# Two moves between VectorE and GpSimd in the second half of a fused attention and two-FFN kernel

## The chip, the cores and the metric

The kernel runs on one core of one Trainium2 chip. The metric is device time in microseconds (us). Four engines matter here: TensorE (PE in the profile's rows) multiplies into PSUM, its weight loads stand as PEld; ScalarE (ACT), VectorE (DVE) and GpSimd (POOL) work on tiles of 128 partitions; SyncE (SP) issues the transfers.

## The reference

`attn(q, k, v)` normalises q and k over 6016 tokens, makes a 256 x 256 softmax over channels and applies it to v. Two feed-forward layers follow, each 256 to 2048 to 256 for 6016 tokens:

```python
h = x @ w_in;  g = h * np.cos(h);                    x = g @ w_out    # first layer
h = x @ w_in;  g = h * (1.0 / (1.0 + np.exp(-h)));   x = g @ w_out    # second layer (SiLU)
```

## The kernel before

The program has three parts. The first (to about 70 us) makes the softmax and folds it into the first layer's w_in. The second (to about 600 us) runs the first layer over 12 blocks of tokens, 4 of 512 and 8 of 496, with 8 pairs of hidden chunks each: 96 units. The third (from about 602 us to the end) is the second layer, and all of the change lies there. Instructions are issued to each engine in the order in which the code is written, and an engine runs its own in that order. A wait is a semaphore set by another engine.

In the third part a 2 x 2 block product is made with seven products instead of eight, P1 to P7, in both directions. Each matmul operand is a pair of tiles, `hi` (rounded to fp32r) and `lo` (the rest), and each product takes three matmuls (hi hi, lo hi, hi lo). For a unit (block b, pair m) the seven products of w_in with x give, after sums in PSUM, four quadrants of h. SiLU of these is the left part of a tile `t` with 8 planes of 128 x c, where c is half a block: 256 for the first four blocks and 248 for the others. From planes 0 to 3 VectorE forms the four others: two by one instruction (line 422, `forms_first`), plane 6 (line 427, called **T3** in this text) and plane 7 (line 428, **T4**, which needs T3). Planes 1 to 7 are then split into `hi` by ScalarE (line 433) and `lo` by VectorE (line 436), each in two instructions: the raw planes 1 to 3 (128 x 3c, 744 columns at c = 248) and the formed planes 4 to 7 (128 x 4c, 992 columns). Then the seven products with w_out add up in two PSUM tiles of the block over its 8 units: the first tile holds P1, P6, P7, P4, the second P5, P3, P2.

The loop runs over slots j (lines 646 to 721), one per unit. In slot j TensorE does P4 and P5 of unit j-1, P1 and P7 of unit j, four w_out products of unit j-3, P3 of j-1, P2 and P6 of j, and the last three w_out products of j-3: 14 products, 42 matmuls. VectorE adds two seeds (lines 660, 661, from PSUM into `t`) for unit j-1, makes `lo` raw and `lo` formed of unit j-2, and then forms_first, T3 and T4 of unit j-1. ScalarE copies P1 and a seed (669, 670), takes the first SiLU (693, needs line 661), makes `hi` formed of unit j-2 (433), two more SiLUs (703, 704), a seed (706), and `hi` raw of unit j-1 (433). P3 adds into the PSUM tile that line 661 reads, so TensorE waits there for VectorE.

When the eighth unit of a block is added up (every 8 slots, here called the boundary), `emit_out` takes the sums: ScalarE copies the first PSUM tile to `q` (line 519), VectorE copies the second (lines 522, 523), and GpSimd makes seven additions within `q` (line 526) and SyncE stores the two halves (lines 530, 534). The additions stand in four steps, one after each of the next slots' T4. GpSimd has no other work in the third part. The last block takes its sums on VectorE.

Of the kernel before, what the change touches and what calls it, by code (L numbers as in the profile page):

```python
# [15 lines left out]
ALU = mybir.AluOpType  # L16
# [47 lines left out]
def attention_then_two_ffns(ctx: ExitStack, tc: tile.TileContext, qk, vT, tau, w_in1, w_out1, w_in2, w_out2, outT):  # L64
# [6 lines left out]
    nc = tc.nc  # L71
# [175 lines left out]
    for g, n in enumerate(GROUPS):  # L247
        c0 = sum(GROUPS[:g])
        t = ep.tile([P, GMAX, 2, C], F32, tag="qk", name=f"qk{g}", bufs=8)
# [47 lines left out]
    for a in range(CH):  # L297
        nc.vector.scalar_tensor_tensor(
            out=E[:, a], in0=S[:, a, :C], scalar=rk[:, a : a + 1], in1=rq, op0=ALU.mult, op1=ALU.mult
# [80 lines left out]
    def emit_first(u, hp):  # L380
        b, m = u
        n = BLOCKS[b][1]
        t = flat(sc.tile([P, NS, HB], F32, tag="t", name=f"t1_{b}_{m}"))
        k = t.bitcast(I32)[:, :, :n]
        nc.scalar.activation(k, hp[:, :, :n], AF.Copy, scale=1.0 / TWO_PI, bias=0.25)  # L385
        nc.vector.scalar_tensor_tensor(  # L386
            out=t[:, :, :n], in0=k, scalar=-TWO_PI, in1=hp[:, :, :n], op0=ALU.mult, op1=ALU.add
        )
        return t
# [34 lines left out]
        )  # L424

    def forms_second(t, c, eng):
        eng.tensor_tensor(out=t[:, 6, :c], in0=t[:, 1, :c], in1=t[:, 5, :c], op=ALU.subtract)  # L427
        eng.tensor_tensor(out=t[:, 7, :c], in0=t[:, 3, :c], in1=t[:, 6, :c], op=ALU.subtract)

    RAW, FORMED = slice(0, 3), slice(3, NU)  # L430
# [4 lines left out]
    def part_lo(t, hi, lo, sl, c):  # L435
        nc.vector.tensor_tensor(  # L436
            out=lo[:, sl, :c], in0=t[:, 1:][:, sl, :c], in1=hi[:, sl, :c].bitcast(F32), op=ALU.subtract
        )
# [26 lines left out]
    def load_x2(b):  # L465
        c = BLOCKS[b][1] // 2
        xparts[2, b] = [xp.tile([P, NU, HB], F32R, tag=f"x{s}", name=f"x2{s}{b}") for s in ("hi", "lo")]
        for t, d in zip(xparts[2, b], xs.pop(b)):
            nc.sync.dma_start(out=t[:, :, :c].bitcast(F32), in_=d)


    def product(out, name, w, x, start, first=True, stop=True):

        ka, kb = PRODUCTS[name]
        for i, (p, r) in enumerate(PASSES):
            nc.tensor.matmul(  # L476
                out,
                w[:, p, ka - 1],
                x[r][:, kb - 1, : out.shape[-1]],
                start=(start and i == 0),  # L480
                stop=(stop and i == 2),
                skip_group_check=True,
            )
# [18 lines left out]
    def emit_out(b):  # L502

        t0, n = BLOCKS[b]
        c = n // 2
        o = state[2, b]
        last = b == NB - 1
        q = qp.tile([P, NU, HB], F32, tag="q", name=f"q{b}", bufs=1)
        p1, p6, p7, p4, p5, p3, p2 = [q[:, i, :c] for i in range(NU)]
        to = outT.rearrange("(a p) (n) -> p a n", p=P)[:, :, t0 : t0 + n].rearrange("p a (j c) -> p a j c", j=2)  # L510
        if last:

            s1, s6, s7, s4, s5, s3, s2 = [o[t][:, k, j, :c] for t, k, j in BANKS.values()]
            eng = nc.vector
            nc.scalar.activation(p1, s1, AF.Copy)
        else:
            s6, s7, s4, s5, s3, s2 = p6, p7, p4, p5, p3, p2
            eng = nc.gpsimd
            nc.scalar.activation(  # L519
                q[:, :4, :c].rearrange("p (k j) c -> p k j c", k=2), o[0][:, :, :, :c], AF.Copy  # L520
            )
            nc.vector.tensor_copy(q[:, 4:6, :c], o[1][:, 0, :, :c])
            nc.vector.tensor_copy(p2, o[1][:, 1, 0, :c])

        def add(out, x, y):
            eng.tensor_tensor(out=out, in0=x, in1=y, op=ALU.add)  # L526

        def first():
            add(p7, p7, s5)
            nc.sync.dma_start(out=to[:, 0], in_=q[:, 2:4, :c])  # L530

        def second():
            add(p2, p1, s2)
            (nc.scalar if last else nc.sync).dma_start(out=to[:, 1], in_=q[:, 5:7, :c])

        return [
            lambda: (add(p6, p1, s6), add(p7, p6, s7)),
            lambda: (add(p4, p7, s4), first()),
            lambda: (add(p6, p6, s5), add(p3, p6, s3)),
            second,  # L540
        ]


# [15 lines left out]
    def fetch(key, to):  # L559
        name, m = key  # L560
        w2[name][m] = to
        nc.sync.dma_start(out=to.bitcast(F32), in_=later.pop(key))
# [3 lines left out]
    def fetch_third():  # L566
        key = third.pop(0)
        fetch(key, as_forms(wp.tile(QUAD, F32R, tag="quad", name=f"{key[0]}_{key[1]}", bufs=8)))
# [7 lines left out]
    for i, u in enumerate(units):  # L576
# [13 lines left out]
        t = emit_first(u, hp)  # L590
# [54 lines left out]
    adds = []  # L645
    for j in range(len(units) + LAG2):
        u, p, o = [units[j - d] if 0 <= j - d < len(units) else None for d in (0, 1, LAG2)]
        if u is not None and u[1] == 2 and u[0] < NB - 1:
            load_x2(u[0] + 1)

        if p is not None:
            k = (j - 1) % 2
            c = BLOCKS[p[0]][1] // 2
            w, x = w2["wi2"][p[1]], xparts[2, p[0]]
            y, z = ys[k][:, :c], zs[k][:, :c]
            p7, u2 = seeds[j - 1]
            t = F[j - 1] = sc.tile([P, NS, HB], F32, tag="t", name=f"t2_{j - 1}")
            product(z, "P4", w, x, start=False)
            product(y, "P5", w, x, start=False)
            nc.vector.tensor_tensor(out=t[:, 1, :c], in0=z, in1=u2, op=ALU.add)  # L660
            nc.vector.tensor_tensor(out=t[:, 0, :c], in0=y, in1=p7, op=ALU.add)  # L661
        if u is not None:
            k2 = j % 2
            c2 = BLOCKS[u[0]][1] // 2
            w_, x_ = w2["wi2"][u[1]], xparts[2, u[0]]
            seeds[j] = [sp.tile([P, HB], F32, tag=s, name=f"{s}_{j}")[:, :c2] for s in ("p7", "u2")]
            product(xx[k2][:, :c2], "P1", w_, x_, start=True)
            product(zs[k2][:, :c2], "P7", w_, x_, start=False)
            nc.scalar.activation(ys[k2][:, :c2], xx[k2][:, :c2], AF.Copy)
            nc.scalar.activation(seeds[j][0], zs[k2][:, :c2], AF.Copy)  # L670
        if j - 2 in hl:
            t_, hi_, lo_, c_ = hl[j - 2]
            part_lo(t_, hi_, lo_, RAW, c_)
        if left:
            v = units[left[0]]
            emit_o1(v, parts.pop(left.pop(0)))
            if v[1] % 2 == 1:
                fetch_third()
            if v[1] == NPAIR - 1:
                steps += emit_x2(v[0])  # L680
        elif steps:
            for _ in range(min(3, len(steps))):
                steps.pop(0)()
            if not steps:
                y_room.close()
                late = ctx.enter_context(tc.tile_pool(name="late", bufs=1))
                for key in FOURTH:
                    fetch(key, late.tile([P, 2, NU, P], F32R, name=f"{key[0]}_{key[1]}"))
        names = list(BANKS)
        if o is not None:  # L690
            emit_o2(o, hl[j - LAG2][1:3], names[:4])
        if p is not None:
            nc.scalar.activation(t[:, 0:2, :c], t[:, 0:2, :c], AF.Silu)  # L693
        if j - 2 in hl:
            part_hi(t_, hi_, FORMED, c_)
            part_lo(t_, hi_, lo_, FORMED, c_)
        if p is not None:
            product(y, "P3", w, x, start=False)
        if u is not None:
            product(xx[k2][:, :c2], "P2", w_, x_, start=False)  # L700
            product(ys[k2][:, :c2], "P6", w_, x_, start=False)
        if p is not None:
            nc.scalar.activation(t[:, 3, :c], xx[k][:, :c], AF.Silu)
            nc.scalar.activation(t[:, 2, :c], y, AF.Silu)
        if u is not None:
            nc.scalar.activation(seeds[j][1], ys[k2][:, :c2], AF.Copy)
        if o is not None:
            emit_o2(o, hl.pop(j - LAG2)[1:3], names[4:])
            if o[1] == NPAIR - 1:
                adds += emit_out(o[0])  # L710
                if o[0] == NB - 1:
                    for step in adds:
                        step()
        if p is not None:
            hi, lo = [sc.tile([P, NU, HB], F32R, tag=s, name=f"{s}2_{j - 1}") for s in ("hi", "lo")]
            hl[j - 1] = (t, hi, lo, c)
            part_hi(t, hi, RAW, c)
            forms_first(t, c)
            forms_second(t, c, nc.vector)
            if adds:  # L720
                adds.pop(0)()


# [25 lines left out]
```

## Time and profile before

| | us |
|---|---|
| median of 3 runs (1133.59 to 1137.45) | 1134.57 |
| the profiled execution | 1134.77 |
| its span, first to last instruction | 1133.0 |
| TensorE busy in the span | 1081.4 (95%) |
| VectorE busy | 939.9 (83%) |
| ScalarE busy | 756.2 (67%) |
| GpSimd busy | 327.6 (29%) |

The span and the time of the same execution differ by 1.77 us. Matmuls are pipelined, so a row of one overlaps the next, and the busy time of TensorE is not its work at peak. A timeline row gives the start, the duration, engine, line, operation, output and inputs, and in brackets how long the engine had stood idle before it and what ended that. The duration of one instruction is longer than the distance to the next when the two don't depend on each other; distances are taken from starts.

### The profile page before, as it was taken

Reading aid. Unit: us, or ns where it says so; the run is one execution under the profiler, and the core shown is the slowest. Engines: PE = TensorE matmul, PEld = TensorE weight load, DVE = VectorE, ACT = ScalarE, POOL = GpSimd, SP = SyncE. Lnnn points to the kernel's source line nnn. Section 1 sums busy time; section 2 is a strip of 40 time slices with the busy share of each in tenths; the row PEclk is TensorE's granted clock in tenths of the full one; section 3 lists DMA queues with packets and bytes.
Section 4 is the critical chain, followed back from the end, with each engine's and each line's share of the span. In section 5 each row is a group of like instructions: output and inputs, shape, how many; then the busy total and the mean of one; then the engine's idle time right before and its main releaser. Section 6 shows DMA issues by size and latency. Waiting matters only on the chain.

```text
span 1133.0 us, 17045 instructions
## 1 busy us (share of the span) xinstructions
PE 1081.4 (95%) x6590; PEld 961.7 (85%) x6590; DVE 939.9 (83%) x1195; ACT 756.2 (67%) x1182; POOL 327.6 (29%) x282
## 2 busy tenths in 40 slices
PE   8888999999999999999998999999999999999997
PEld 7756788888888888888887999889989999899897
DVE  6899897887897888877675888888888888888887
ACT  6555666666666666665665777677677677778675
POOL 2268554564463564501000020220220220220220
PEclk9999999999999999999999999999999999999999
DMA  9712222324315324301275521022022022022000
GB/s 359 281 50 81 75 84 70 116 69 167 135 37 183 110 74 155 123 32 50 65 274 209 196 82 67 20 82 64 20 82 64 19 82 64 19 82 64 19 19 19
DMA packets 56528, 109.49 MB, mean 97 GB/s; under 512 B 2816, under 2 KB 37632, under 8 KB 56448
## 3 DMA queue, kind: packets, MB, share of 16 engines
q1 hardware_dynamic: 56176, 108.15, 28.1%
q8 instruction: 52, 0.85, 0.3%
q10 hardware_dynamic: 272, 0.25, 0.1%
q14 instruction: 28, 0.23, 0.1%
HBM read 68.75 MB, written 39.65 MB: 96 GB/s over the span
## 4 chain that ended last, share of the span: by engine, by line
PE 76%; DVE 15%; issue 4%; ACT 3%; DMA 1%; SPq 0%; DVEq 0%; ACTq 0%
PE o L412 21%; PE h L373 21%; PE o L476 15%; PE xz L476 9%; PE ys L476 8%; DVE t L422 2%; DVE acc L267 2%; DVE t L427 2%; ACT hi L433 2%; PE pw L334 1%; DVE t L661 1%; DVE lo L402 1%; ACT t L693 1%; DVE t L386 1%; DVE t L394 1%
## 5 line engine op out<-in xcount | busy, mean ns | idle before, releaser
L436 DVE TENSOR_TENSOR lo<-t,hi 128x744 fp32r<-128x744 f32 (+1 forms) x192 | 213.4, 1112 | 67.0 <-ACT hi L433 67.0
L476 PE MATMUL o<-hi,wo 128*128 128x248 f32 (+1 forms) x1344 | 246.1, 281 | 0.0
L526 POOL TENSOR_TENSOR q<-q 128x248 f32<-128x248 f32 (+1 forms) x77 | 76.3, 1001 | 498.7 <-ACT q L519 495.3
L476 PEld LDWEIGHTS o<-hi,wo 128*128 128x128 f32 x1344 | 207.8, 192 | 0.0
L373 PE MATMUL h<-xhi,wa 128*128 128x496 f32 (+1 forms) x768 | 206.1, 390 | 1.6 <-DVE wa L342 1.6
L412 PE MATMUL o<-hi,wo 128*128 128x496 f32 (+1 forms) x768 | 206.7, 391 | 0.0
L476 PE MATMUL o<-lo,wo 128*128 128x248 f32 (+1 forms) x672 | 189.2, 281 | 1.4 <-DVE lo L436 1.3
L433 ACT ACTIVATE hi<-t 128x744 fp32r<-128x744 f32 (+1 forms) x192 | 178.9, 932 | 13.5 <-PE o L476 11.0
L386 DVE SCALAR_TENSOR_TENSOR t<-t,h 128x992 f32<-128x992 int32 (+1 forms) x96 | 114.9, 1197 | 82.2 <-ACT t L385 81.8
L385 ACT ACTIVATE t<-h 128x992 int32<-128x992 f32 (+1 forms) x96 | 96.8, 1008 | 128.3 <-PE h L373 124.3
L373 PEld LDWEIGHTS h<-xhi,wa 128*128 128x128 f32 x768 | 144.0, 188 | 33.4 <-ACT wa L340 2.4
L412 PEld LDWEIGHTS o<-hi,wo 128*128 128x128 f32 x768 | 144.8, 189 | 30.8
L393 ACT ACTIVATE t<-t,half_pi 128x992 f32<-128x992 f32 (+1 forms) x96 | 109.1, 1136 | 66.4 <-DVE t L386 66.4
L476 PE MATMUL ys<-x2hi,wi 128*128 128x248 f32 (+1 forms) x576 | 122.5, 294 | 28.4 <-DVE t L661 25.9
L476 PE MATMUL xz<-x2hi,wi 128*128 128x248 f32 (+1 forms) x768 | 148.7, 281 | 0.0
L402 DVE TENSOR_TENSOR lo<-t,hi 128x992 fp32r<-128x992 f32 (+1 forms) x96 | 133.8, 1394 | 1.2 <-ACT hi L401 1.2
L476 PEld LDWEIGHTS o<-lo,wo 128*128 128x128 f32 x672 | 128.8, 192 | 1.9 <-DVE lo L436 1.9
L412 PE MATMUL o<-lo,wo 128*128 128x496 f32 (+1 forms) x384 | 119.5, 393 | 6.2 <-DVE lo L402 6.2
L394 DVE TENSOR_TENSOR t<-h,t 128x992 f32<-128x992 f32 (+1 forms) x96 | 115.1, 1199 | 6.9 <-ACT t L393 1.2
L476 PEld LDWEIGHTS ys<-x2hi,wi 128*128 128x128 f32 x576 | 88.8, 192 | 35.9 <-DVE t L661 29.7
L476 PEld LDWEIGHTS xz<-x2hi,wi 128*128 128x128 f32 x768 | 119.2, 192 | 0.1
L373 PE MATMUL h<-xlo,wa 128*128 128x496 f32 (+1 forms) x384 | 118.3, 389 | 0.0
(111 smaller groups left out, 1685.6 us busy)
## 6 DMA issues: line engine op xcount, KB each, us to landing
qk<-qk_dram SPq DMA_DIRECT2D x22, 512.0 KB, 7.7
raw_wo<-w_out_dram SPq DMA_DIRECT2D x16, 512.0 KB, 5.0
xshi<-yhi SPq DMA_DIRECT2D x8, 868.0 KB, 6.4
xslo<-ylo SPq DMA_DIRECT2D x8, 868.0 KB, 6.9
x2hi<-xshi SPq DMA_DIRECT2D x8, 868.0 KB, 5.2
x2lo<-xslo SPq DMA_DIRECT2D x8, 868.0 KB, 7.2
wo_dram<-stage_wo SPq DMA_DIRECT2D x7, 896.0 KB, 4.7
wo<-wo_dram SPq DMA_DIRECT2D x7, 896.0 KB, 7.5
```

The source lines that it names most:

```text
L267: nc.vector.tensor_tensor(out=acc[:, :n], in0=acc[:, :n], in1=sq[:, :n], op=ALU.add)
L373: nc.tensor.matmul(hp[:, s, :n], lhsT, rhs, start=(i == 0), stop=(i == len(todo) - 1))
L385: nc.scalar.activation(k, hp[:, :, :n], AF.Copy, scale=1.0 / TWO_PI, bias=0.25)
L386: nc.vector.scalar_tensor_tensor(out=t[:, :, :n], in0=k, scalar=-TWO_PI, in1=hp[:, :, :n], op0=ALU.mult, op1=ALU.add)
L393: nc.scalar.activation(t[:, :, :n], t[:, :, :n], AF.Sin, bias=half_pi)
L394: nc.vector.tensor_tensor(out=t[:, :, :n], in0=hp[:, :, :n], in1=t[:, :, :n], op=ALU.mult)
L402: nc.vector.tensor_tensor(out=lo[:, :, :n], in0=t[:, :, :n], in1=hi[:, :, :n].bitcast(F32), op=ALU.subtract)
L412: nc.tensor.matmul(o[:, e, :n], wo1_at(i, f)[:, e * P : (e + 1) * P], parts[k][:, s, :n], start=(f == 0 and (i, k) == PASSES[0]), stop=(f ...
L433: nc.scalar.activation(hi[:, sl, :c], t[:, 1:][:, sl, :c], AF.Copy)
L436: nc.vector.tensor_tensor(out=lo[:, sl, :c], in0=t[:, 1:][:, sl, :c], in1=hi[:, sl, :c].bitcast(F32), op=ALU.subtract)
L476: nc.tensor.matmul(out, w[:, p, ka - 1], x[r][:, kb - 1, : out.shape[-1]], start=(start and i == 0), stop=(stop and i == 2), skip_group_ch ...
L526: eng.tensor_tensor(out=out, in0=x, in1=y, op=ALU.add)
```

## The change

T4 goes from VectorE to GpSimd in all 96 slots of the third part (T3 stays on VectorE; the other use of `forms_second`, in `emit_x2` on the first layer's output, keeps both on VectorE). The seven additions of a block's sums go from GpSimd to VectorE. The two copies of the second PSUM tile leave the boundary slot: `emit_out` now returns six steps, the copies first, and the loop runs one step per slot right after lines 658 and 659 (660 and 661 before).

```diff
     def forms_second(t, c, eng):
-        eng.tensor_tensor(out=t[:, 6, :c], in0=t[:, 1, :c], in1=t[:, 5, :c], op=ALU.subtract)
+        nc.vector.tensor_tensor(out=t[:, 6, :c], in0=t[:, 1, :c], in1=t[:, 5, :c], op=ALU.subtract)
         eng.tensor_tensor(out=t[:, 7, :c], in0=t[:, 3, :c], in1=t[:, 6, :c], op=ALU.subtract)
...
-            nc.vector.tensor_copy(q[:, 4:6, :c], o[1][:, 0, :, :c])
-            nc.vector.tensor_copy(p2, o[1][:, 1, 0, :c])
+
+        def second_tile():
+            if not last:
+                nc.vector.tensor_copy(q[:, 4:6, :c], o[1][:, 0, :, :c])
+                nc.vector.tensor_copy(p2, o[1][:, 1, 0, :c])
 
         def add(out, x, y):
-            eng.tensor_tensor(out=out, in0=x, in1=y, op=ALU.add)
...
+            nc.vector.tensor_tensor(out=out, in0=x, in1=y, op=ALU.add)
+
+        def store(e, sl, eng=nc.sync):
+            eng.dma_start(out=to[:, e], in_=q[:, sl, :c])
 
         return [
+            second_tile,
             lambda: (add(p6, p1, s6), add(p7, p6, s7)),
-            lambda: (add(p4, p7, s4), first()),
+            lambda: add(p4, p7, s4),
+            lambda: (add(p7, p7, s5), store(0, slice(2, 4))),
             lambda: (add(p6, p6, s5), add(p3, p6, s3)),
-            second,
+            lambda: (add(p2, p1, s2), store(1, slice(5, 7), nc.scalar if last else nc.sync)),
         ]
...
             nc.vector.tensor_tensor(out=t[:, 0, :c], in0=y, in1=p7, op=ALU.add)
+        if adds:
+            adds.pop(0)()
         if u is not None:
...
             forms_first(t, c)
-            forms_second(t, c, nc.vector)
-            if adds:
-                adds.pop(0)()
+            forms_second(t, c, nc.gpsimd)
```

VectorE at the boundary after block 7, program order before the change: the last instructions of one slot and the first of the next (`t2_65` is the `t` of unit 65, `o2_7_1` the second PSUM tile of block 7, `q7` the block's sums).

```order
L436 TENSOR_TENSOR lo2_64_8565<-t2_64_8508,hi2_64_8564 128x4x248
L522 COPY q7_8630<-o2_7_1_8148 128x2x248
L523 COPY q7_8630<-o2_7_1_8148 128x248
L422 TENSOR_TENSOR t2_65_8574<-t2_65_8574 128x2x248
L427 TENSOR_TENSOR t2_65_8574<-t2_65_8574 128x248
L428 TENSOR_TENSOR t2_65_8574<-t2_65_8574 128x248
L660 TENSOR_TENSOR t2_66_8642<-xz0_4372,u2_66_8584 128x248
L661 TENSOR_TENSOR t2_66_8642<-ys0_4370,p7_66_8583 128x248
L436 TENSOR_TENSOR lo2_65_8635<-t2_65_8574,hi2_65_8634 128x3x248
L436 TENSOR_TENSOR lo2_65_8635<-t2_65_8574,hi2_65_8634 128x4x248
```

The same place after the change.

```order
L436 TENSOR_TENSOR lo2_64_8565<-t2_64_8508,hi2_64_8564 128x4x248
L422 TENSOR_TENSOR t2_65_8574<-t2_65_8574 128x2x248
L427 TENSOR_TENSOR t2_65_8574<-t2_65_8574 128x248
L658 TENSOR_TENSOR t2_66_8638<-xz0_4372,u2_66_8584 128x248
L659 TENSOR_TENSOR t2_66_8638<-ys0_4370,p7_66_8583 128x248
L523 COPY q7_8630<-o2_7_1_8146 128x2x248
L524 COPY q7_8630<-o2_7_1_8146 128x248
L436 TENSOR_TENSOR lo2_65_8633<-t2_65_8574,hi2_65_8632 128x3x248
L436 TENSOR_TENSOR lo2_65_8633<-t2_65_8574,hi2_65_8632 128x4x248
```

T4 is gone from VectorE in this slot and in every other, and the copies stand two seed additions later, ahead of `lo` raw. The next slots have one or two rows of line 527 (the additions) at the place of the copies.

ScalarE in the slot after, before the change, with the engines that each instruction waits for.

```order
L693 ACTIVATE t2_66_8642<-t2_66_8642 128x2x248 [waits DVE_49]
L433 ACTIVATE hi2_65_8634<-t2_65_8574 128x4x248
L703 ACTIVATE t2_66_8642<-xz0_4372 128x248
L704 ACTIVATE t2_66_8642<-ys0_4370 128x248 [waits PE_49]
L706 ACTIVATE u2_67_8652<-ys1_4371 128x248 [waits PE_49]
```

The same place after the change.

```order
L693 ACTIVATE t2_66_8638<-t2_66_8638 128x2x248 [waits DVE_49]
L433 ACTIVATE hi2_65_8632<-t2_65_8574 128x4x248 [waits Pool_49]
L703 ACTIVATE t2_66_8638<-xz0_4372 128x248
L704 ACTIVATE t2_66_8638<-ys0_4370 128x248 [waits PE_49]
L706 ACTIVATE u2_67_8650<-ys1_4371 128x248 [waits PE_49]
```

`hi` formed now waits for GpSimd's T4; behind it on ScalarE stand two SiLUs and a seed copy, and on VectorE `lo` formed waits for it.

## Rows read from the trace of the kernel before

**Rows 1.** Stretches: length, busy PE, PEld, DVE, ACT, POOL, then PEclk, DMA, GB/s.

```profile
70.00:600.00 530.00, 523.75 (x2288) 428.45 (x2287) 439.00 (x419) 335.12 (x346) 227.87 (x183) 1.00 0.31 106
...
662.00:1088.00 426.00, 403.96 (x3359) 398.31 (x3358) 363.48 (x581) 312.51 (x650) 69.43 (x70) 0.98 0.16 51
...
797.70:801.00 3.30, 3.30 (x18) 3.30 (x17) 3.08 (x4) 2.23 (x5) 2.69 (x2) 0.50 0.19 69
```

**Rows 2.** Timeline of VectorE, one slot within a block, c = 248.

```profile
805.34 0.67 DVE L422 TENSOR_TENSOR t<-t 128x496 f32<-128x496 f32 x1
806.04 0.42 DVE L427 TENSOR_TENSOR t<-t 128x248 f32<-128x248 f32 x1
806.49 0.42 DVE L428 TENSOR_TENSOR t<-t 128x248 f32<-128x248 f32 x1
806.82 0.41 DVE L660 TENSOR_TENSOR t<-xz,u 128x248 f32<-128x248 f32 x1
807.15 0.41 DVE L661 TENSOR_TENSOR t<-ys,p 128x248 f32<-128x248 f32 x1
807.47 0.92 DVE L436 TENSOR_TENSOR lo<-t,hi 128x744 fp32r<-128x744 f32 x1
809.16 1.19 DVE L436 TENSOR_TENSOR lo<-t,hi 128x992 fp32r<-128x992 f32 x1 [0.77 <-ACT hi L433]
810.27 0.67 DVE L422 TENSOR_TENSOR t<-t 128x496 f32<-128x496 f32 x1
```

**Rows 3.** Timeline of ScalarE in the same slot.

```profile
807.59 0.62 ACT L693 ACTIVATE t<-t 128x496 f32<-128x496 f32 x1
808.11 1.02 ACT L433 ACTIVATE hi<-t 128x992 fp32r<-128x992 f32 x1
```

**Rows 4.** Chain of waits: 12 w_out matmuls in a row, c = 256.

```profile
719.99 1.41 PE o L476 x12
```

**Rows 5.** The same, c = 248.

```profile
811.61 1.36 PE o L476 x12
```

**Rows 6.** First and last copy of a block's first PSUM tile (source view).

```profile
L519 ACT ACTIVATE q<-o x11: 1009/1013/1037, 662.0 to 1088.5; 128x992 f32<-128x992 f32 x7, 128x1024 f32<-128x1024 f32 x4
```

**Rows 7.** Timeline of VectorE at a boundary, GpSimd adding from 835.59.

```profile
834.97 0.67 DVE L522 COPY q<-o 128x496 f32<-128x496 f32 x1
835.55 0.41 DVE L523 COPY q<-o 128x248 f32<-128x248 f32 x1
835.87 0.97 DVE L422 TENSOR_TENSOR t<-t 128x496 f32<-128x496 f32 x1
836.88 0.82 DVE L427 TENSOR_TENSOR t<-t 128x248 f32<-128x248 f32 x1
...
838.45 0.40 DVE L660 TENSOR_TENSOR t<-xz,u 128x248 f32<-128x248 f32 x1
...
839.10 1.46 DVE L436 TENSOR_TENSOR lo<-t,hi 128x744 fp32r<-128x744 f32 x1
```

**Rows 8.** Timeline of ScalarE there.

```profile
834.50 1.01 ACT L519 ACTIVATE q<-o 128x992 f32<-128x992 f32 x1
```

**Rows 9.** Timeline of GpSimd there, four of the seven additions, one by one.

```profile
835.59 0.72 POOL L526 TENSOR_TENSOR q<-q 128x248 f32<-128x248 f32 x1 [35.20 <-ACT q L519]
...
838.33 0.76 POOL L526 TENSOR_TENSOR q<-q 128x248 f32<-128x248 f32 x1
...
839.85 1.30 POOL L526 TENSOR_TENSOR q<-q 128x248 f32<-128x248 f32 x1
...
841.10 1.67 POOL L526 TENSOR_TENSOR q<-q 128x248 f32<-128x248 f32 x1
```

**Rows 10.** Timeline of TensorE there.

```profile
839.24 0.51 PE L476 MATMUL ys<-x2hi,wi 128*128 128x248 f32 x2 [1.86 <-DVE t L661]
```

**Rows 11.** Waits, 612 to 1133 us: who waited for whom, total, times, longest.

```profile
PE ys L476 <- DVE t L661: 25.9, 19, 2.0
...
ACT hi L433 <- DVE t L428: 1.4, 1, 1.4
```

More of the change, by code (lines that the diff above doesn't have):

```diff
@@ L510, in emit_out @@
         to = outT.rearrange("(a p) (n) -> p a n", p=P)[:, :, t0 : t0 + n].rearrange("p a (j c) -> p a j c", j=2)
+        s6, s7, s4, s5, s3, s2 = p6, p7, p4, p5, p3, p2
         if last:
             s1, s6, s7, s4, s5, s3, s2 = [o[t][:, k, j, :c] for t, k, j in BANKS.values()]
-            eng = nc.vector
             nc.scalar.activation(p1, s1, AF.Copy)
         else:
-            s6, s7, s4, s5, s3, s2 = p6, p7, p4, p5, p3, p2
-            eng = nc.gpsimd
             nc.scalar.activation(
@@ L521, in emit_out @@
             )
-            nc.vector.tensor_copy(q[:, 4:6, :c], o[1][:, 0, :, :c])
-            nc.vector.tensor_copy(p2, o[1][:, 1, 0, :c])
+        def second_tile():
+            if not last:
+                nc.vector.tensor_copy(q[:, 4:6, :c], o[1][:, 0, :, :c])
+                nc.vector.tensor_copy(p2, o[1][:, 1, 0, :c])
         def add(out, x, y):
-            eng.tensor_tensor(out=out, in0=x, in1=y, op=ALU.add)
[L528 to L534, printed above, removed]
+            nc.vector.tensor_tensor(out=out, in0=x, in1=y, op=ALU.add)
+        def store(e, sl, eng=nc.sync):
+            eng.dma_start(out=to[:, e], in_=q[:, sl, :c])
         return [
+            second_tile,
             lambda: (add(p6, p1, s6), add(p7, p6, s7)),
-            lambda: (add(p4, p7, s4), first()),
+            lambda: add(p4, p7, s4),
+            lambda: (add(p7, p7, s5), store(0, slice(2, 4))),
             lambda: (add(p6, p6, s5), add(p3, p6, s3)),
-            second,
+            lambda: (add(p2, p1, s2), store(1, slice(5, 7), nc.scalar if last else nc.sync)),
         ]
```

## The prediction

> **What bounds the kernel now.** I read three views: stretches of the span, to see which part loses time; the timelines of VectorE and ScalarE through one slot, to see which work repeats without slack; the timelines at a boundary, to see what breaks the pace.
>
> The stretches say where to look. In the first layer TensorE is busy for 523.75 of 530 us at a granted clock of 1.00, so nothing is to be had there. In the 426 us of the second layer it is busy for 403.96, and its clock is 0.98 on average: for 3.3 us after one boundary it is 0.50, which is 1.2 of 2.4 GHz [rows 1].
>
> A slot within a block is a loop over two engines. Count from the start of T3. T4 starts 0.45 later, L660 0.33 after that, L661 another 0.33, the SiLU that needs L661 0.44 later, `hi` formed 0.52 after it, `lo` formed 1.05 after that, forms_first 1.11 later and the next T3 0.70 behind it [rows 2, 3]. The sum is 4.93, which is also the distance of the two forms_first. In this ring VectorE stands idle once, 0.77 us for `hi` formed [rows 2]. TensorE's work of a slot is shorter: 12 matmuls take 1.36 at c = 248, so 42 take 4.76; at c = 256 they take 3.5 x 1.41 = 4.94 [rows 4, 5]. So TensorE gains on VectorE within a block, which is why the chain of waits names TensorE there, and stands still at the next boundary: 1.86 for L661 [rows 10], 25.9 us in 19 such waits over the part [rows 11]. After these the clock drops.
>
> At the boundary the ring is longer. The two copies take 0.58 and 0.32, and while GpSimd adds, forms_first lasts 0.97 instead of 0.67, T3 0.82 instead of 0.42, `lo` raw 1.46 instead of 0.92 [rows 2, 7]. L660, whose inputs are one in PSUM and one in SBUF, keeps its 0.40, and so does the copy (0.41).
>
> From the first boundary's copy at 662.0 to the eleventh's at 1088.5 there are 80 slots in 426.5 us [rows 6], 5.33 each. TensorE's work in them is 23 x 4.94 + 57 x 4.76 = 385. I conclude that the VectorE/ScalarE ring, not TensorE, sets the time of the second layer.
>
> **T4 leaves the ring.** T3 to L660 becomes 0.33 instead of 0.45 + 0.33, since L660 does not need T3 as T4 does. The ring becomes 4.93 - 0.45 = 4.48, under TensorE's 4.76.
>
> **T4 on GpSimd.** T3 ends at 0.42. GpSimd began 0.08 after what it waited for (834.50 + 1.01 against 835.59 [rows 8, 9]), so T4 begins at 0.50. `hi` formed would begin at 0.33 + 0.33 + 0.44 + 0.52 = 1.62. T4 has 1.12 us to hide in. The trace has no T4 there, but 77 additions on GpSimd of its shape (49 at c = 248): 0.76 beside L660, 1.30 beside `lo` raw and 1.67 beside two-input work alone [rows 9]. T4 would run beside L660 and L661 until 0.98, so I take 0.76: done at 1.26, hidden by the SiLU. At 1.30 the ring would be 4.48 + 0.18 = 4.66, still under 4.76; at 1.67 it would be 5.03. Where TensorE paces the slots, L661 and the SiLU wait for it and T4 has more room. The wait is on ScalarE, and `lo` formed would be late with it.
>
> What speaks against it is a rule of the Trainium skill, SBUF — State Buffer, section "Who interferes with whom": a VectorE instruction with two SBUF inputs and a GpSimd instruction that reads SBUF take one port pair by exclusive lock, and the second to issue blocks until the first is done. The rows agree that such pairs cost both engines and that L660 is spared; they don't show a full block, since an addition beside `lo` raw took 1.30 and not 0.92 + 0.76. By the rule T4, first at the port, would hold up the instruction behind L661 by 0.28, which is inside the idle 0.77.
>
> Against it stands also the Trainium skill's GPSIMD Engine Reference, section "Performance versus the Vector engine": elementwise work belongs on VectorE, which is about twice as fast. The rows agree, 0.42 against 0.76 [rows 2, 9]; an estimate by the page's ratio of 1.96 would be 0.82. Neither uses up 1.12, so the sum is the same by both.
>
> **Additions on VectorE.** A step is placed behind L661, ahead of `lo` raw. Their price, from the like rows L660 and T3: 0.33 for one, 0.45 + 0.33 = 0.78 for two in a chain, and up to 0.28 more because T4 is still at the port from 0.98 to 1.26 [rows 2]. The copies cost 0.90 and aren't slowed [rows 7]. The cover is the 0.77 that VectorE waits for `hi` formed. Over it stick 0.13 for the copies and 0.29 for each of two pairs: 0.7 us per block. So a block's ring is 8 x 4.48 + 0.7 = 36.5 against TensorE's 38.1. At nothing hidden, seven additions at 0.41 and 0.90 make 3.8, and the ring is 39.6.
>
> **What goes with them.** The boundary's copies no longer stand before forms_first, and GpSimd's 7 us beside VectorE's two-input work are gone. The second PSUM tile is freed later by about a slot's first half; TensorE writes it anew only with the last 9 of the slot's 42 matmuls, 27 matmuls or 3.1 us behind P5. L661 needs P5, and the copies end 0.33 + 0.90 behind L661's start, so about 1.5 us are to spare and I cost it at nothing; without that cover it would be at most the 0.90 per boundary. The stores leave three slots later, the second still two slots (9.5 us) before `q` is written again; SyncE's other transfers stay in their order. ScalarE's copy at the boundary (1.01) now lies in the time in which `hi` raw waits for TensorE.
>
> **The sum.** Against the profiled execution, 1134.77, which is 0.2 above the median:
> - 80 slots at TensorE's pace: 426.5 - 385 = 41.5 saved.
> - the slots before the first boundary: 10 x (4.93 - 4.76) is 1.7; first-layer leftovers run there, so I take 1.
> - after the last boundary: its stall of 1.9 and the half clock behind it (3.3 us at 0.50, 1.7 lost) go, 3.6.
> - the very last unit: `hi` formed already waits for T4 there, 1.4 us, with nothing to hide it [rows 11]. T4 on GpSimd beside `lo` raw ends 0.4 to 1.0 later; I take 0.6 more.
> - left over: 0.1 to 0.2 at each of 11 boundaries, 1.5.
>
> 1134.8 - 41.5 - 1.0 - 3.6 + 0.6 + 1.5 = 1090.8; I say **1091**.
>
> **Rivals.**
> - *Work is not covered, VectorE stays the bound.* Either the additions aren't hidden (39.6 a block against 38.1: 1.5 x 11 = 17, 1108), or T4 takes 1.67 each time (8 x 5.03 + 0.7 = 40.9: 2.8 x 11 = 31, 1122). For it: slack is only 0.28 a slot. Against: T4's neighbours are L660 and L661, and rows 9 show 0.76 beside them. Chance 0.18.
> - *TensorE is the bound already.* The chain of waits gives it most of the part. Then its stalls are absorbed elsewhere and nothing changes, about 1134. Against: 5.33 a slot for work of 4.76 to 4.94. Chance 0.03.
> - *T4 starts too late and loses the port: slower.* If GpSimd begins after 0.98 (0.56 or more behind T3, not 0.08) and `lo` raw blocks it to the end at 1.90, T4 is done at 1.90 + 0.76 = 2.66 and `hi` formed moves from 1.62 to there. The ring is 4.48 + 1.04 = 5.52, above the 5.33 of now: 80 x 0.19 = 15 more, 1150. It decides from a T4 that ends 0.85 after 1.62, at 2.47. For it: 839.85, where an addition met `lo` raw and took 1.30, so the two do hurt each other [rows 9]. Against: the 0.08, and that 1.30 is less than 0.92 + 0.76. The lock of SBUF — State Buffer in the Trainium skill is the rule that would make it so. Chance 0.06.
>
> **How the numbers follow.** The forecast, TensorE paces the second layer, has 0.73 and its own range 1086 to 1097: lower if no boundary costs anything and the first slots save more, higher at T4 of 1.30 in the slots with two additions. Eight in ten must take in the uncovered additions, so 1086 to 1110. A difference under 0.3% (3.4 us) can't be told from none. Faster takes the forecast and the first rival, 0.91; same 0.03; slower 0.06.
>
> **What would show it.** Right: forms_first to forms_first about 4.76 within blocks of c = 248 and no 7 us slots; VectorE idle for TensorE in front of L658 or ScalarE in front of its copies; waits of TensorE for L659 near zero; granted clock 1.00 through the layer; T4 near 0.76 and no wait of `hi` formed for it but the last. Wrong: T4 of 1.3 or more, ScalarE waiting for GpSimd in every slot, `lo` raw well above 0.92 with VectorE never idle, or TensorE waiting for ScalarE's seed copies in the place of L659.

## The result and the profile after

The changed kernel takes 1088.01 us (median of 4 runs, 1086.78 to 1089.08), the kernel before 1134.13 beside it. The ratio is 0.9587, 95% interval 0.9566 to 0.9609: faster by 4.1%. The forecast was 1091, range 1086 to 1110. The profiled execution of after took 1088.41, its span is 1086.6.

The first view of after is the stretch between the first and the last boundary, in the columns of [rows 1].

```profile
662.00:1040.00 378.00, 378.00 (x3303) 378.00 (x3302) 338.93 (x562) 300.24 (x639) 57.36 (x79) 1.00 0.18 58
```

TensorE is busy all the time at a granted clock of 1.00, where it was busy for 403.96 of 426 at 0.98. That alone is not proof that it sets the pace: records of matmuls overlap, and the kernel of the second experiment shows 387.99 of 388 while it is 16 us slower.

```profile
662.00:1050.00 388.00, 387.99 (x3274) 382.11 (x3273) 354.82 (x637) 304.93 (x633) 0.00 (x0) 1.00 0.18 56
```

The starts of the matmuls are better evidence. In the changed kernel they follow each other without a gap from 662 to 1040 us, some 0.12 apart at c = 256 and 0.11 at c = 248. In the second experiment's kernel nearly every slot has a gap of 0.1 to 0.2, at the product that waits for VectorE's second seed (L659). The copies of the first PSUM tile mark the blocks; this is the source view that answers to [rows 6].

```profile
L517 ACT ACTIVATE q<-o x11: 1029/1033/1059, 660.5 to 1045.4; 128x992 f32<-128x992 f32 x7, 128x1024 f32<-128x1024 f32 x4
```

The 80 slots take 384.9 us. TensorE's own work in them had been worked out from matmul distances as 385; that the two agree so closely is partly luck, since a block took 39.2 instead of 39.5 at c = 256 and 38.2 instead of 38.1 at c = 248. TensorE now paces the layer, and no gap is left there.

The timeline of VectorE through one slot, to be laid beside [rows 2]:

```profile
792.62 0.67 DVE L422 TENSOR_TENSOR t<-t 128x496 f32<-128x496 f32 x1
793.32 0.42 DVE L427 TENSOR_TENSOR t<-t 128x248 f32<-128x248 f32 x1
793.66 0.41 DVE L658 TENSOR_TENSOR t<-xz,u 128x248 f32<-128x248 f32 x1
793.99 0.41 DVE L659 TENSOR_TENSOR t<-ys,p 128x248 f32<-128x248 f32 x1
794.31 0.61 DVE L527 TENSOR_TENSOR q<-q 128x256 f32<-128x256 f32 x1
794.84 0.92 DVE L436 TENSOR_TENSOR lo<-t,hi 128x744 fp32r<-128x744 f32 x1
796.27 1.19 DVE L436 TENSOR_TENSOR lo<-t,hi 128x992 fp32r<-128x992 f32 x1 [0.51 <-ACT hi L433]
797.38 0.67 DVE L422 TENSOR_TENSOR t<-t 128x496 f32<-128x496 f32 x1
```

The slot is 4.76, not 4.93. An addition (256 columns, since it belongs to the block before) lies between L659 and `lo` raw, and VectorE still stands idle 0.51 for `hi` formed. ScalarE and GpSimd in the same slot:

```profile
794.69 0.62 ACT L693 ACTIVATE t<-t 128x496 f32<-128x496 f32 x1
795.20 1.03 ACT L433 ACTIVATE hi<-t 128x992 fp32r<-128x992 f32 x1
```

```profile
793.91 0.73 POOL L428 TENSOR_TENSOR t<-t 128x248 f32<-128x248 f32 x1 [4.04 <-DVE t L427]
```

T4 begins 0.17 after T3's end and is done at 794.64, 0.56 before `hi` formed, which doesn't wait for it. The waits of after, 600 to 1087 us (who waited for whom, total, times, longest):

```profile
DVE lo L436 <- ACT hi L433: 44.4, 73, 1.7
ACT hi L433 <- PE o L476: 39.3, 80, 0.8
...
ACT hi L433 <- POOL t L428: 2.3, 1, 2.3
...
PE ys L476 <- DVE t L659: 0.3, 1, 0.3
```

TensorE's 25.9 us for VectorE [rows 11] have become 0.3, and ScalarE now waits for TensorE 80 times. GpSimd is waited for once in 96 slots.

### The profile page after: what moved, and what is told of

It is laid out like the page before. It is cut to its first block, busy times and chain, and to the rows that moved or that the text cites. A ratio compares the mean times of both kernels' runs of the same rounds, so it can differ in the third digit from the quotient of the medians.

```text
span 1086.6 us, 17004 instructions
## 1 busy us (share of the span) xinstructions
PE 1059.1 (97%) x6590; PEld 945.5 (87%) x6590; DVE 917.8 (84%) x1176; ACT 748.4 (69%) x1182; POOL 321.1 (30%) x301
## 4 chain that ended last, share of the span: by engine, by line
PE 90%; DVE 6%; ACT 1%; DMA 1%; issue 0%; SPq 0%; POOLq 0%; DVEq 0%; ACTq 0%
PE o L412 22%; PE h L373 22%; PE o L476 21%; PE xz L476 12%; PE ys L476 9%; PE S L239 3%; DVE lo L402 1%; PE pw L334 1%; DVE t L386 1%; DVE t L394 1%; DMA raw_w<-w_in_dram 1%; DVE wv_wo L136 1%; DVE wv_wo L140 0%; DVE wv_wo L137 0%; DMA qk<-qk_dram 0%
## 5 line engine op out<-in xcount | busy, mean ns | idle before, releaser
L436 DVE TENSOR_TENSOR lo<-t,hi 128x744 fp32r<-128x744 f32 (+1 forms) x192 | 210.3, 1097 | 45.9 <-ACT hi L433 44.4
L476 PE MATMUL o<-hi,wo 128*128 128x248 f32 (+1 forms) x1344 | 241.2, 278 | 1.1 <-ACT hi L433 1.1
L428 POOL TENSOR_TENSOR t<-t 128x248 f32<-128x248 f32 (+1 forms) x96 | 70.3, 732 | 484.4 <-DVE t L427 426.1
L433 ACT ACTIVATE hi<-t 128x744 fp32r<-128x744 f32 (+1 forms) x192 | 180.7, 941 | 41.6 <-PE o L476 39.3
L476 PEld LDWEIGHTS o<-hi,wo 128*128 128x128 f32 x1344 | 204.0, 189 | 1.3 <-ACT hi L433 1.3
L476 PE MATMUL o<-lo,wo 128*128 128x248 f32 (+1 forms) x672 | 186.9, 278 | 1.2 <-DVE lo L436 1.2
L412 PEld LDWEIGHTS o<-hi,wo 128*128 128x128 f32 x768 | 144.6, 188 | 30.7
L476 PEld LDWEIGHTS xz<-x2hi,wi 128*128 128x128 f32 x768 | 116.8, 189 | 0.2
L476 PE MATMUL ys<-x2hi,wi 128*128 128x248 f32 (+1 forms) x576 | 113.4, 278 | 3.1 <-ACT u L706 2.7
L476 PE MATMUL xz<-x2lo,wi 128*128 128x248 f32 (+1 forms) x384 | 106.7, 278 | 0.0
```

The source lines that it names most:

```text
L412: nc.tensor.matmul(o[:, e, :n], wo1_at(i, f)[:, e * P : (e + 1) * P], parts[k][:, s, :n], start=(f == 0 and (i, k) == PASSES[0]), stop=(f ...
L433: nc.scalar.activation(hi[:, sl, :c], t[:, 1:][:, sl, :c], AF.Copy)
L436: nc.vector.tensor_tensor(out=lo[:, sl, :c], in0=t[:, 1:][:, sl, :c], in1=hi[:, sl, :c].bitcast(F32), op=ALU.subtract)
L476: nc.tensor.matmul(out, w[:, p, ka - 1], x[r][:, kb - 1, : out.shape[-1]], start=(start and i == 0), stop=(stop and i == 2), skip_group_ch ...
```

## Experiments

Two theories were at stake. **The ring**: the loop T3, L660, L661, SiLU, `hi` formed, `lo` formed, forms_first, is the bound, and less T4 it is under TensorE's time, and what is put into VectorE's idle 0.77 is free. **The sums**: what counts is that GpSimd no longer adds beside VectorE. The 80 slots between the first and the last copy of a first PSUM tile serve as measure: 426.5 us before, 384.9 after.

**T4 alone.** The kernel before with T4 on GpSimd, and nothing else.

```diff
     def forms_second(t, c, eng):
-        eng.tensor_tensor(out=t[:, 6, :c], in0=t[:, 1, :c], in1=t[:, 5, :c], op=ALU.subtract)
+        nc.vector.tensor_tensor(out=t[:, 6, :c], in0=t[:, 1, :c], in1=t[:, 5, :c], op=ALU.subtract)
...
-            forms_second(t, c, nc.vector)
+            forms_second(t, c, nc.gpsimd)
             if adds:
                 adds.pop(0)()
```

> T4 goes to GpSimd, the additions stay on GpSimd in their four steps and the two copies stay at the boundary. If the ring of VectorE and ScalarE is the bound and T4's place in it is the main thing: 4 slots of a block at 4.48, 4 slots in which the additions now run behind T4, beside lo raw and lo formed, at 4.8 to 5.0, and 0.90 for the copies, so 37.9 to 38.8 per block against TensorE's 38.1: 1089 to 1096 us. If the additions beside VectorE's work are the main cost: 2 to 2.5 us per block stay, 1110 to 1116 us.

Measured: 1101.73 us, ratio 0.9708 (0.9694 to 0.9723). It hits neither range. T4 alone brings 33 of the 46 us, the 80 slots take 397.0. The timelines of VectorE and GpSimd at a boundary show the rest:

```profile
901.11 0.68 DVE L522 COPY q<-o 128x496 f32<-128x496 f32 x1 [0.15 <-PE o L476]
901.70 0.41 DVE L523 COPY q<-o 128x248 f32<-128x248 f32 x1
902.02 0.67 DVE L422 TENSOR_TENSOR t<-t 128x496 f32<-128x496 f32 x1
902.72 0.42 DVE L427 TENSOR_TENSOR t<-t 128x248 f32<-128x248 f32 x1
...
906.50 1.19 DVE L422 TENSOR_TENSOR t<-t 128x496 f32<-128x496 f32 x1
907.73 0.42 DVE L427 TENSOR_TENSOR t<-t 128x248 f32<-128x248 f32 x1
```

```profile
903.31 0.71 POOL L428 TENSOR_TENSOR t<-t 128x248 f32<-128x248 f32 x1 [5.26 <-DVE t L427]
903.98 1.41 POOL L526 TENSOR_TENSOR q<-q 128x248 f32<-128x248 f32 x1
...
905.47 1.69 POOL L526 TENSOR_TENSOR q<-q 128x248 f32<-128x248 f32 x1
```

From forms_first to forms_first is 4.48 here (902.02 to 906.50), the ring's length as worked out. Then the second addition, queued behind T4, lies beside forms_first, which lasts 1.19 for 0.67, and T3 comes 5.01 after the last. Three such slots, with 5.01 each, are about what the expectation had put in (4.8 to 5.0). The boundary slot and the free ones are what it had too cheap. A block at c = 248 takes 39.3: the boundary slot 5.92 from T3 to T3 instead of 4.48 + 0.90, three slots of 5.01, two of 4.49, then 4.56 and 4.78. VectorE runs at 4.48 only until it has caught up with TensorE; the boundary slot therefore starts from TensorE's pace, and its copies wait another 0.15 for TensorE's last product.

**The sums and the copies alone.** The changed kernel with T4 on VectorE.

```diff
-            forms_second(t, c, nc.gpsimd)
+            forms_second(t, c, nc.vector)
```

> The additions go to VectorE in the five slots and the copies into the next slot, T4 stays on VectorE. By the ring: 8 slots of 4.93 and 0.15 that sticks out, 39.6 per block at c = 248 against TensorE's 38.1, and 5.06 a slot against 4.94 at c = 256: about 15 us over the changed kernel, 1103 us, TensorE waiting a little for VectorE in every slot. If taking GpSimd's additions off is the whole gain: 1088 to 1091. If T4 is the whole gain: 1125 or more.

Measured: 1103.89 us, ratio 0.9726 (0.9711 to 0.974): by the ring. VectorE's timeline in a slot with the copies (GpSimd has nothing to do in this kernel):

```profile
902.68 0.67 DVE L422 TENSOR_TENSOR t<-t 128x496 f32<-128x496 f32 x1
903.39 0.42 DVE L427 TENSOR_TENSOR t<-t 128x248 f32<-128x248 f32 x1
903.84 0.42 DVE L428 TENSOR_TENSOR t<-t 128x248 f32<-128x248 f32 x1
904.18 0.41 DVE L658 TENSOR_TENSOR t<-xz,u 128x248 f32<-128x248 f32 x1
904.50 0.41 DVE L659 TENSOR_TENSOR t<-ys,p 128x248 f32<-128x248 f32 x1
904.83 0.66 DVE L523 COPY q<-o 128x496 f32<-128x496 f32 x1
...
907.67 0.67 DVE L422 TENSOR_TENSOR t<-t 128x496 f32<-128x496 f32 x1
```

The copies make the slot 4.99 where the ring without them is 4.93: nearly all of their 0.90 is hidden. The 80 slots take 398.3 us. So each half alone gives some 31 to 33 us and both 46: the halves shorten the same ring, and TensorE's work is the floor that cuts off the rest. How the 31 us divide between the additions and the copies while T4 is still on VectorE was not tried.

**The copies back at the boundary**, all else as changed.

```diff
         return [
-            second_tile,
...
+        second_tile()
+        return [
```

> The changed kernel with the two copies back in the boundary slot, ahead of forms_first. By the ring: 8 x 4.48 + 0.90 + 0.6 for the pairs of additions = 37.3 per block, under 38.1, so no change: 1088 to 1090. If a delay of 0.90 at the boundary makes TensorE stand still and its clock fall: 11 x (about 0.5 + 1.7) more, 1110 or so.

Measured: 1093.48 us, ratio 0.9639 (0.9623 to 0.9655), 5 us slower than the changed kernel and neither theory's number. The 80 slots take 389.8, 0.5 more per block. In VectorE's timeline the copies cost 0.91 and a wait of 0.16 for TensorE's last product:

```profile
896.38 0.68 DVE L523 COPY q<-o 128x496 f32<-128x496 f32 x1 [0.16 <-PE o L476]
896.97 0.41 DVE L524 COPY q<-o 128x248 f32<-128x248 f32 x1
897.29 0.67 DVE L422 TENSOR_TENSOR t<-t 128x496 f32<-128x496 f32 x1
...
898.65 0.41 DVE L659 TENSOR_TENSOR t<-ys,p 128x248 f32<-128x248 f32 x1
```

The expectation compared a block's ring, 37.3, with TensorE's 38.1. That is the wrong sum: VectorE can't save up time in the slots where it waits for TensorE, so a delay in one slot is only taken up as far as TensorE's slack behind that slot reaches. TensorE's timeline shows the rest: P3 waits for L659, which ends at 899.06, and begins only at 899.11.

```profile
898.81 0.27 PE L476 MATMUL o<-lo,wo 128*128 128x248 f32 x1
899.11 0.50 PE L476 MATMUL ys<-x2hi,wi 128*128 128x248 f32 x2
899.45 0.28 PE L476 MATMUL ys<-x2lo,wi 128*128 128x248 f32 x1
```

From the first row to the third lie three matmuls, 0.34 at 0.11 each, and here 0.64: 0.30 is lost, once in every block of c = 248, which takes 38.5 to 38.6 instead of 38.2. At c = 256 a block takes 40.0 instead of 39.2; there such gaps make some 0.27, and the rest stays open. The granted clock was 1.00 from 662 to 1040 us, so the fall that the other theory priced is excluded.

**T4 twice** on GpSimd, the second time with the same result.

```diff
+        for _ in range(2 if eng is nc.gpsimd else 1):
-        eng.tensor_tensor(out=t[:, 7, :c], in0=t[:, 3, :c], in1=t[:, 6, :c], op=ALU.subtract)
+            eng.tensor_tensor(out=t[:, 7, :c], in0=t[:, 3, :c], in1=t[:, 6, :c], op=ALU.subtract)
```

> The changed kernel with T4 done twice on GpSimd, the second time with the same result, in every slot: how late may T4 be? In the changed kernel hi formed begins 1.88 us behind T3. If GpSimd, first at the port, keeps 0.76 for both, the second ends 2.2 behind T3, hi formed is 0.3 late and the ring is 5.06: 1110 to 1115. If the second takes 1.30 beside lo raw, it ends at 2.73 and the ring is 5.59: 1155 to 1165. If T4 has more room than the ring says: 1088.

Measured: 1129.41 us, ratio 0.9956 (0.9941 to 0.9971). Both cases occur, in different slots. First a slot without an addition, VectorE, then the second T4 on GpSimd, then `hi` formed on ScalarE:

```profile
915.26 0.42 DVE L427 TENSOR_TENSOR t<-t 128x248 f32<-128x248 f32 x1
...
916.24 1.09 DVE L437 TENSOR_TENSOR lo<-t,hi 128x744 fp32r<-128x744 f32 x1
...
920.82 0.42 DVE L427 TENSOR_TENSOR t<-t 128x248 f32<-128x248 f32 x1
```

```profile
916.62 1.29 POOL L429 TENSOR_TENSOR t<-t 128x248 f32<-128x248 f32 x1
```

```profile
917.94 1.03 ACT L434 ACTIVATE hi<-t 128x992 fp32r<-128x992 f32 x1 [0.96 <-POOL t L429]
```

T3 to T3 is 5.56, against 5.59 expected. `lo` raw lasts 1.09 instead of 0.92 because the first T4, from 915.82, still runs when it starts. Then a slot with an addition, which holds `lo` raw back until the second T4 has begun:

```profile
930.87 0.42 DVE L427 TENSOR_TENSOR t<-t 128x248 f32<-128x248 f32 x1
...
931.85 0.57 DVE L528 TENSOR_TENSOR q<-q 128x248 f32<-128x248 f32 x1
932.34 1.45 DVE L437 TENSOR_TENSOR lo<-t,hi 128x744 fp32r<-128x744 f32 x1
...
935.91 0.42 DVE L427 TENSOR_TENSOR t<-t 128x248 f32<-128x248 f32 x1
```

```profile
932.23 0.77 POOL L429 TENSOR_TENSOR t<-t 128x248 f32<-128x248 f32 x1
```

Here it is 5.04, against 5.06. Six slots of a block are of the second kind and two of the first. A lateness of T4 goes into the ring nearly one for one (`hi` formed begins 2.68 behind T3 in the first slot, where the ring has 1.62, and the slot is 1.08 over 4.48), and a T4 twice as long costs 41 us: the change works because one T4 ends before `hi` formed can begin.

**The additions back on GpSimd**, in the new order of steps, T4 there as well.

```diff
         def add(out, x, y):
-            nc.vector.tensor_tensor(out=out, in0=x, in1=y, op=ALU.add)
+            (nc.vector if last else nc.gpsimd).tensor_tensor(out=out, in0=x, in1=y, op=ALU.add)
```

> The changed kernel with the additions back on GpSimd but in the new order of steps: copies in the next slot, then 2, 1, 1, 2 and 1 additions, each step in GpSimd's queue behind a T4. In the run with T4 alone a step of two additions reached into forms_first (1.19 for 0.67) and gave slots of 5.01. By the ring only the two steps of two do so here, 0.25 above TensorE's 4.76 and with free slots between them, so VectorE's slack takes them: 1088 to 1090. If additions on GpSimd cost by their number, 7 a block, the time is nearer to the run with T4 alone: 1094 to 1101.

Measured: 1088.81 us (1086.87 to 1089.76), ratio 0.9599 (0.9586 to 0.9612): the same as the changed kernel, 1088.32 beside it. The stretch shows GpSimd with 2.5 times the work, VectorE with less, and TensorE as before:

```profile
662.00:1040.00 378.00, 378.00 (x3303) 378.00 (x3302) 320.79 (x491) 302.47 (x640) 143.24 (x149) 1.00 0.19 58
```

A step of two additions gives VectorE a slot of 5.12 to 5.15 from T3 to T3, more than the 5.01 expected, but the slots behind it take 4.49 and 4.67, and TensorE's matmuls have no gap from 662 to 1040 us. So with T4 on GpSimd and the new order of steps, the move of the additions to VectorE earns nothing. What separates this kernel from that with T4 alone, 13 us, is the order: fewer additions per slot and the copies in the next slot. The copies' place was priced above at 5; that the spreading makes the rest is a difference, not a run of its own.

**The last T4 on VectorE**, a version that might beat both, with the changed kernel beside it on the same chip.

```diff
-            forms_second(t, c, nc.gpsimd)
+            forms_second(t, c, nc.vector if j == len(units) else nc.gpsimd)
```

> The changed kernel with the T4 of the very last unit on VectorE, as it was before. Nothing follows that unit in which GpSimd's slower T4 could hide, and beside lo raw it took 1.26: hi formed waited 2.3 us there against 1.4 before. If that wait is on the path to the end, 0.9 us less than the changed kernel; if the end is set otherwise, the same time.

> The changed kernel once more, beside the other two on one chip: 1087 to 1089.

Measured: 1087.26 us (1085.91 to 1087.74) and 1088.32 (1086.87 to 1088.82), ratios 0.9586 (0.9573 to 0.9599) and 0.9594 (0.9581 to 0.9608). The medians differ by 1.1 us, the runs overlap; by the runs alone it is not shown. The profile shows a mechanism of that size. In the changed kernel the last T4 and `hi` formed, on GpSimd and ScalarE, with VectorE's `lo` raw, which starts ahead of T4:

```profile
1075.30 0.93 DVE L436 TENSOR_TENSOR lo<-t,hi 128x744 fp32r<-128x744 f32 x1
```

```profile
1075.55 1.25 POOL L428 TENSOR_TENSOR t<-t 128x248 f32<-128x248 f32 x1 [3.77 <-DVE t L427]
```

```profile
1076.84 1.03 ACT L433 ACTIVATE hi<-t 128x992 fp32r<-128x992 f32 x1 [2.33 <-POOL t L428]
```

In the new one the wait is that of the kernel before, 1.4 (waits, 1040 us to the end):

```profile
ACT hi L433 <- DVE t L428: 1.4, 1, 1.4
```

From the last copy of a first PSUM tile to the end of the span it takes 40.2 us instead of the 41.2 of both profiles of the changed kernel.

## Why the prediction was right, and where it was not

**The bound.** That the ring of VectorE and ScalarE set the pace, against the chain of waits which named TensorE for most of the part, is shown: the ring without T4 was measured at 4.48 and the ring with T4 and no GpSimd work at 4.93, both as read off [rows 2, 3], each shortening of it paid until TensorE's 4.76 was reached, and with both TensorE's matmuls run without a gap.

**The terms.** The 80 slots were put at 41.5 and gave 41.6. The slots before the first boundary were put at 1 and gave 1.5 (the first copy stands at 660.5 instead of 662.0). From the last copy to the end 3.0 net was forecast, and it was 3.3 (44.5 to 41.2). Of it T4 in the last unit cost 0.9, not 0.6. The 1.5 left over at the boundaries, which I had put in without a row for it, did not exist. That is half of the 3 us by which the forecast was too high; the first slots make 0.5, the end 0.3, and the profiled execution lies 0.4 above the median. The clock's part in the prediction, that it drops after TensorE's stalls, held after about half of them only; see the last section.

**T4's cover.** It was put at 0.76 in a room of 1.12. It took 0.72 to 0.73 and began 0.17, not 0.08, after T3; it was done 0.56 before `hi` formed began. The instruction behind L659 was held up by some 0.2 (an addition took 0.61, against 0.41 at 248 columns in the second experiment, where GpSimd is idle), where the prediction had up to 0.28. Twice the length was too much, as the rival's arithmetic had it.

**The lock.** Here a step failed, though the forecast did not hang on it. I had read from [rows 9] that an addition beside `lo` raw took 1.30, not 0.92 + 0.76, and that the rows therefore don't show a full block. In the run with T4 twice, the second T4 began at 916.62, 0.38 after `lo` raw, which ended at 917.33; it ended 0.58 after that. Where it began first, it took 0.77 and `lo` raw 1.45 instead of 0.92; it ended 0.79 after T4 did. So whoever begins second stands still but for some 0.15 at its start, nearly what the Trainium skill says in SBUF — State Buffer, section "Who interferes with whom". The 1.30 was the same: `lo` raw had itself been held up and ended at 840.56, 0.71 after the addition's start [rows 7, 9]. The slower rival's price, 2.66 for a T4 that loses the port, was about right; what kept it away is that T4 begins while VectorE is at L658 and L659, beside which it took 0.72. In the last unit those two are missing, `lo` raw starts 0.25 ahead of T4, and T4 took 1.25.

**The additions.** They were costed as hidden in VectorE's idle time, which held. But the prediction also counted the end of GpSimd's 7 us beside VectorE among the gains. The run with the additions on GpSimd shows that this has no price once the steps are spread and T4 has left the ring.

**The copies.** They were costed at nothing in the slot after beyond the 0.13 that sticks out, and that held: no gap of TensorE is left. At the boundary the expectation costed them at nothing too. That was not so: 5 us.

## What to carry to other kernels

Where two engines hand work to and fro every slot, add up the ring of their starts and compare it with the slowest engine's own work; the chain of waits can name an engine that merely catches up in between. Work taken out of the ring pays until the next engine's floor, and two changes that shorten the same ring don't add up. A lump of work in one slot in eight costs time even where the average has room, so spread it over slots and place it where its engine waits anyway.

## What the runs showed of the hardware that was not expected

The fall of TensorE's clock did not follow every stall. In the kernel before, TensorE stood still 1.91 us at one boundary and 1.86 at the next [rows 10]:

```profile
796.79 0.51 PE L476 MATMUL ys<-x2hi,wi 128*128 128x248 f32 x2 [1.91 <-DVE t L661]
```

The stretches from boundary to boundary, both with c = 248:

```profile
792.00:834.00 42.00, 40.09 (x334) 39.73 (x333) 35.75 (x59) 30.56 (x65) 6.98 (x7) 0.96 0.18 56
834.00:876.00 42.00, 39.51 (x336) 38.63 (x335) 35.95 (x58) 30.86 (x66) 6.87 (x7) 1.00 0.18 55
```

After the first stall the granted clock was 0.50 (1.2 GHz) for 3.3 us [rows 1], after the second it stayed at 1.00 (2.4 GHz). Why is not shown. Of the ten blocks between the first and the last boundary five have a mean clock of 0.96 and five 1.00. At c = 248 the former take 42.4 to 42.5 us from copy to copy and the latter 42.2: VectorE's ring set the length, and a slower TensorE mostly used up slack. So the clock cost about 0.2 us a block there, and in the changed kernel, without the stalls, it stays at 1.00 from 662 to 1040 us.

An instruction of GpSimd and a two-input one of VectorE, both on SBUF, run one after the other but for some 0.15 us, and the order of their starts decides which of them is late. Where `lo` raw began 0.25 ahead, it took 0.93 and T4 1.25 (the last unit of the changed kernel); where T4 began 0.11 ahead, it took 0.77 and `lo` raw 1.45 (T4 twice).
